# Another order for the first batch of a fused chunked-attention and MLP kernel

## The chip, the core and the metric

The kernel runs on one core of one Trainium2 chip. The core has five engines that run side by side and meet at semaphores: TensorE (PE: matmuls, and transposes done as matmuls), VectorE (DVE), ScalarE (ACT), GpSimd (POOL) and SyncE (SP). Loads and stores are issued from the queues of SP, ACT and POOL and carried out by 16 DMA engines. The metric is the device time of one execution in microseconds. Lower is better.

## The reference

Inputs are q, k, v of shape 4 x 8 x 768 x 64 (batch, heads, sequence, head size), eight memory rows per head for keys and values, and the weights of an MLP (512 to 2048 to 512). The sequence is cut into chunks of 32 queries. A chunk sees the memory rows, 16 rows to its left, its own 32 and 8 to its right. Then comes an MLP with a snake activation.

```python
for c in range(768 // 32):
    l, r = max(0, 32*c - 16), min(768, 32*c + 32 + 8)
    k_full = concat(mem_k, k[:, :, l:r]);  v_full = concat(mem_v, v[:, :, l:r])
    a = softmax(0.125 * q[:, :, 32*c:32*c + 32] @ k_full.T)
    out[:, :, 32*c:32*c + 32] = a @ v_full
x = out with heads side by side              # 3072 x 512
h = x @ w_in                                 # 3072 x 2048
g = h + sin(alpha * h)**2 / (alpha + 1e-9)
y = g @ w_out                                # 3072 x 512
```

## The kernel before

The attention of a batch is computed in blocks of 96 queries, three chunks each, which share one window of 128 keys: 64 rows of K, 8 memory rows, 56 rows of K (`vw` holds V in the same windows). Eight such blocks make a sequence.

Batch 0 has a form of its own, in *units*: a unit is a pair of heads (0 to 3) and a half of the sequence (0 or 1), four blocks each, so there are eight units. In the names below "10" is pair 1, half 0. K and Q of pairs 0, 1 and 2 arrive in fp32 by the queues of SP and ACT (`kq_f`, lines 748 and 756 to 758) and are cast to bf16 (`do_a`, line 683). Pair 3 of both arrives cast by GpSimd's queue (`load_one`, line 191). Every pair is turned on TensorE (`turn`, line 312) and copied from PSUM into `kT` and `qT` (lines 323 and 332). Then, unit by unit, `u_scores` makes the mask and the scores in a pair of PSUM banks (lines 350 and 358) and their exponentials `pt` on ScalarE (line 365). `u_values` multiplies by V (line 377), and `normed` divides on VectorE (a reciprocal, line 386, and a multiplication, line 387) into `x_blk`. `u_turn` turns `x_blk` back on TensorE (line 399) and copies it into `xT` on ScalarE or VectorE (line 402). V comes by GpSimd's queue, one pair of heads per word in two or three transfers (`load_v`, lines 204 to 217), and `put_memv` writes the eight memory rows of V into every window (line 224).

After that there are four stages, one for each batch. A stage computes the batch's MLP and, between its matmuls, the attention of the next batch. The first MLP matmul has 16 tiles of 128 rows of d_ff. A tile has two halves of 384 tokens and each half accumulates four parts (kt 0 to 3, one per pair of heads; line 457) in a pair of PSUM banks. Then come a sine on ScalarE (line 472), a square on one of three engines (lines 477 and 480) and the sum `gT` on VectorE (line 484). The second matmul is at line 495 and its stores at line 505.

The order of all this is written out by hand in the table `WORDS`: one text for the front (batch 0's attention) and one for each stage. Each word calls a method `do_` plus its first letter, and every engine executes its instructions in the order in which the words emit them. The words that matter here are:

- y and z: zero matmuls that keep TensorE busy, of 128 and 512 columns (lines 725 and 719)
- Cb, Ck, Cl, Cm and others: constants (masks, memory keys, alpha); Cv, Cz, Cp, Cs are memsets on GpSimd
- a4A: cast of tile 4 (0 to 3 are K's pairs, 4 to 7 Q's) on ScalarE; a last letter V means VectorE
- k0, l0: turns of K's and Q's pair 0; K0A, L0V: their copies, with the engine
- s10, v10, T10, t10: scores, values and turn of unit 10, the copy on ScalarE (T) or VectorE (t)
- V024: V of batch 0, heads 2 and 3; m0: the memory rows of V; dq068: a load of Q, batch 0, heads 6 and 7
- I02: w_in tiles 0 and 1; Ws, We: loading of the sine or the exponential table on ScalarE
- p0 and P0: parts 0 to 2 of MLP tile 0, first and second half; b0 and h0: the rest of that half

PSUM has eight banks of 512 fp32 columns. `Banks` hands out single banks and pairs, the one that was given back first ahead of the others, so another order of the words gives other banks.

The front before loads V of pairs 1, 0, 3, 2 in this order and takes the values in the order 11, 10, 01, 00, 31, 30, 21, 20.

Of the kernel before, what the change touches and what calls it, by code (L numbers as in the profile page):

```python
# [17 lines left out]
ALU = mybir.AluOpType  # L18
# [1 line left out]

WORDS = (
    (
# [4 lines left out]
    ),  # L27
    (
# [93 lines left out]
def kernel(  # L122
# [12 lines left out]
    nc = tc.nc  # L135
# [5 lines left out]
    HP = H // 2  # L141
    FT = d_ff // P
    KT = d_model // P
# [173 lines left out]
    def copier(eng):  # L317
        return {"A": nc.scalar.copy, "V": nc.vector.tensor_copy, "P": nc.gpsimd.tensor_copy}[eng]
# [136 lines left out]
    def half_tile(t, hf, k0=0, k1=4):  # L455
        for kt in range(k0, k1):
            nc.tensor.matmul(  # L457
                t["hT"][:, hf, 0:HALF],
                w_in_sb[:, kt, P * t["ft"]:P * t["ft"] + P],
                t["xT"][:, kt, HALF * hf:HALF * hf + HALF],  # L460
                start=(kt == 0), stop=(kt == KT - 1),
            )

    def opened(ft, xT):
        hT, bs = banks.pair()
        return {"ft": ft, "xT": xT, "hT": hT, "bs": bs, "from": [0, 0]}
# [66 lines left out]
    kq = (k_bf, q_bf)  # L533
    todo = [(hp, half) for hp in range(HP) for half in range(2)]

    class Stage:
# [29 lines left out]
        def early(self, a, hf):  # L566
# [3 lines left out]
            half_tile(t, hf, 0, 3)  # L570
            t["from"][hf] = 3

        def do_p(self, a):
            self.early(a, 0)

# [106 lines left out]

        def do_a(self, a):
            hp = int(a[0]) % HP
            dst = kq[int(a[0]) // HP]
            copier(a[1])(  # L686
                dst[:, 2 * hp:2 * hp + 2].rearrange("p h r d -> p h (r d)"), kq_f[int(a[0])][:]
            )

        def do_C(self, a):  # L690
            consts_of[a]()
# [50 lines left out]
    kq_f = [mlp.tile([P, 2, 6 * D], F32, name="kq_f", tag=t) for t in ("u", "s2") * 4]  # L742
# [146 lines left out]
```

## Time and profile before

| | us |
|---|---|
| median of 3 runs | 214.41 (214.40 to 214.45) |
| profiled execution | 214.68 |
| its span, first to last instruction | 212.8 |
| first MLP matmul of batch 0 starts | 24.78 |

| engine | busy us | share of the span |
|---|---|---|
| TensorE | 204.9 | 96% |
| ScalarE | 143.7 | 68% |
| VectorE | 139.9 | 66% |
| GpSimd | 100.9 | 47% |

In the profile's rows a timeline row gives start, duration, engine, line, operation, tile written and tiles read, and in brackets the idle time before it and what ended that. "q" behind an engine's name is its sequencer, which issues DMAs. A row of a group ends with busy time, mean ns of one, and idle time before it with its releasers. A row of DMA issues gives count, size and the microseconds from issue to landing. A row of the chain of waits gives start, duration and what held the end back at that time. Neighbouring rows of one kind are merged ("x8").

### The profile page before, as it was taken

The page shows a single profiled execution, that of the slowest core. Times are in us where ns is not written, and L with a number is a line of the kernel's source. Part 1 is how long each engine was busy: PE and PEld are TensorE (multiplying, and loading weights), DVE is VectorE, ACT ScalarE, POOL GpSimd, SP SyncE. Part 2 cuts the span into 40 slices and gives each one's busy share as a digit, 9 for nine tenths or more (in the row PEclk, how much of TensorE's full clock was granted, in tenths as well). Part 3 has the DMA queues.
Part 4 walks back from the last instruction along what each step waited for, and adds up shares of the span by engine and source line. Part 5 has one row for each costly group of instructions (what it writes and reads, how often), then busy time and mean ns, then how long its engine had stood idle before and what let it go on. Part 6 is the DMA issues. An engine that isn't in the chain of part 4 may idle for free.

```text
span 212.8 us, 4568 instructions
## 1 busy us (share of the span) xinstructions
PE 204.9 (96%) x1772; PEld 118.1 (55%) x1772; DVE 139.9 (66%) x210; ACT 143.7 (68%) x229; POOL 100.9 (47%) x142
## 2 busy tenths in 40 slices
PE   7879999999999999999999999999999999999994
PEld 7456665565455556555455555554555555554453
DVE  4788788999452749976766649897247187865010
ACT  2579898978848469968837199887856189891110
POOL 8998605589697297109795048664000022200000
PEclk9999999999999999999999999999999999999999
DMA  5999999999999999999999259999944400000312
GB/s 156 332 158 139 212 207 204 205 139 183 131 160 155 176 114 129 121 144 146 146 152 183 74 125 125 137 157 133 134 104 107 137 0 0 3 2 0 148 52 99
DMA packets 95853, 27.82 MB, mean 131 GB/s; under 512 B 84808, under 2 KB 92376, under 8 KB 95832
## 3 DMA queue, kind: packets, MB, share of 16 engines
q0 software_dynamic: 69152, 13.64, 89.3%
q1 hardware_dynamic: 25720, 12.68, 29.6%
q10 hardware_dynamic: 960, 1.21, 1.7%
q8 instruction: 14, 0.23, 0.6%
q14 instruction: 7, 0.06, 0.1%
HBM read 29.66 MB, written 6.29 MB: 169 GB/s over the span
## 4 chain that ended last, share of the span: by engine, by line
PE 78%; DVE 8%; ACT 5%; DMA 4%; issue 3%; SPq 1%; DVEq 0%; ACTq 0%
PE ps L495 39%; PE ps L457 30%; DMA kq_f<-in_k_dram 4%; PE ps L447 3%; DVE gT L484 2%; PE ps L418 2%; DVE x_blk L387 2%; DVE s L480 2%; ACT s L477 2%; PE ps L399 1%; ACT pt L365 1%; PE ps L312 1%; ACT u L472 1%; DVE q_bf L686 1%; DVE rinv L386 0%
## 5 line engine op out<-in xcount | busy, mean ns | idle before, releaser
L495 PE MATMUL ps<-w_out_sb,gT 128*128 128x512 bf16 (+1 forms) x400 | 89.1, 371 | 0.0
L457 PE MATMUL ps<-xT,w_in_sb 128*128 128x384 bf16 x512 | 85.9, 326 | 0.6 <-DVE gT L484 0.4
L484 DVE SCALAR_TENSOR_TENSOR gT<-s,inv_alpha,ps 128x768 bf16<-128x768 f32 x64 | 63.1, 1012 | 12.3 <-ACT s L477 5.2
L457 PEld LDWEIGHTS <-w_in_sb 128*128 128x128 bf16 x512 | 49.7, 98 | 35.2 <-issue 2.0
L472 ACT ACTIVATE u<-ps,alpha_sb 128x768 f32<-128x768 f32 x64 | 56.6, 894 | 16.9 <-PE ps L457 14.4
L495 PEld LDWEIGHTS <-gT 128*128 128x128 bf16 x400 | 37.1, 98 | 37.1 <-DVE gT L484 0.2
L480 POOL TENSOR_TENSOR s<-u 128x768 f32<-128x768 f32 x11 | 17.2, 1568 | 67.2 <-ACT u L472 56.4
L432 ACT ACTIVATE pt<-ps,biasm 128x256 bf16<-128x256 f32 x72 | 27.1, 488 | 10.5 <-PE ps L418 10.5
L502 DVE COPY o_sb<-ps 128x512 f32<-128x512 f32 (+1 forms) x15 | 10.0, 669 | 27.6 <-PE ps L495 25.7
L480 DVE TENSOR_TENSOR s<-u 128x768 f32<-128x768 f32 x23 | 21.9, 953 | 7.6 <-ACT u L472 7.5
L477 ACT ACTIVATE s<-u 128x768 f32<-128x768 f32 x30 | 25.0, 841 | 0.5
L387 DVE TENSOR_TENSOR x_blk<-ps,rinv 96x512 bf16<-96x512 f32 x32 | 22.0, 687 | 1.1
L502 ACT COPY o_sb<-ps 128x512 f32<-128x512 f32 (+1 forms) x10 | 5.7, 572 | 22.0 <-PE ps L495 22.0
L208 POOL DMA_DIRECT2D vw<-in_v_dram x13 | 12.0, 926 | 6.3 <-PE ps L399 5.4
L386 DVE RECIPROCAL rinv<-ps 96x8 f32<-96x8 f32 x32 | 6.4, 199 | 13.1 <-PE ps L447 12.7
L215 POOL DMA_DIRECT2D vw<-in_v_dram x13 | 13.3, 1024 | 1.6 <-DMA vw<-in_v_dram 1.6
L274 POOL DMA_DIRECT2D kst<-in_k_dram x16 | 13.0, 815 | 1.8 <-DMA vw<-in_v_dram 1.2
L268 POOL DMA_DIRECT2D kst<-in_k_dram x16 | 11.1, 691 | 2.1 <-DMA kst<-in_k_dram 1.0
L281 POOL DMA_DIRECT2D q_bf<-in_q_dram x12 | 10.7, 911 | 0.0
L402 ACT COPY xT<-ps 128x384 bf16<-128x384 bf16 x10 | 5.0, 496 | 8.2 <-PE ps L399 8.2
L447 PEld LDWEIGHTS <-pt 128*128 128x128 bf16 x192 | 8.2, 97 | 4.2 <-ACT pt L432 0.3
L447 PE MATMUL ps<-vw,pt 128*128 128x65 bf16 x192 | 8.9, 193 | 0.0
(83 smaller groups left out, 140.7 us busy)
## 6 DMA issues: line engine op xcount, KB each, us to landing
out_dram<-o_sb SPq DMA_DIRECT2D x23, 256.0 KB, 2.2
q_bf<-in_q_dram POOLq DMA_DIRECT2D x12, 128.0 KB, 7.7
kq_f<-in_k_dram SPq DMA_DIRECT2D x3, 384.0 KB, 6.2
kq_f<-in_q_dram ACTq DMA_DIRECT2D x3, 384.0 KB, 7.9
w_in_sb<-in_moe_w_in_dram POOLq DMA_DIRECT2D x1, 1152.0 KB, 12.9
vw<-in_v_dram POOLq DMA_DIRECT2D x7, 128.0 KB, 7.7
vw<-in_v_dram POOLq DMA_DIRECT2D x8, 112.0 KB, 8.1
kst<-in_k_dram POOLq DMA_DIRECT2D x14, 64.0 KB, 5.5
```

The source lines that it names most:

```text
L215: nc.gpsimd.dma_start(vw[72:128, c0:hi, 0:D], win(vflat, base + QW * c0 + 48, hi - c0, 56))
L274: nc.gpsimd.dma_start(kst[72:72 + n, j, :].rearrange("p (h d) -> p h d", d=D), k[b, :, QW * j + 48:QW * j + 48 + n, :].rearrange("h p d -> ...
L387: nc.vector.tensor_tensor(out=x_blk[:].rearrange("p g e d -> p e g d"), in0=otv[0:QW, :, :, 0:D], in1=rinv[:].unsqueeze(3).to_broadcast([Q ...
L432: nc.scalar.activation(pt[:, 0:H * QW].rearrange("p (g e c) -> p g e c", g=2, e=4)[:, :, :, 32 * m:32 * m + 32], sc[:, :, 0:4 * QW].rearra ...
L447: nc.tensor.matmul(otv[:, e, hp, :], pt[:, QW * i:QW * i + P], vws[b % 2][:, 2 * hp + e, j, 0:D + 1],)
L457: nc.tensor.matmul(t["hT"][:, hf, 0:HALF], w_in_sb[:, kt, P * t["ft"]:P * t["ft"] + P], t["xT"][:, kt, HALF * hf:HALF * hf + HALF], start= ...
L472: nc.scalar.activation(t["u"][:], t["hT"][:, :, 0:HALF], ACTF.Sin, scale=alpha_sb[:, ft:ft + 1])
L477: nc.scalar.activation(s2[:], u[:], ACTF.Square)
L480: e.tensor_tensor(out=s2[:], in0=u[:], in1=u[:], op=ALU.mult)
L484: nc.vector.scalar_tensor_tensor(out=gT[:, ft, :].rearrange("p (e c) -> p e c", e=2), in0=t["s2"][:], scalar=inv_alpha[:, ft:ft + 1], in1= ...
L495: nc.tensor.matmul(o[:, c0:c1], gT[:, ft, P * s:P * s + P], w_out_sb[:, ft, c0:c1], start=(ft == 0), stop=(ft == FT - 1),)
L502: copier(state["engines"][state["o"] % len(state["engines"])])(o_sb[:, c0:c1], o[:, c0:c1])
```

## The change

Only the front's order, one cast's form and one unused method are changed. The texts of the four stages stay as they are.

- V is loaded by pairs 0, 1, 2, 3, and the values are taken in that order.
- K's pair 0 and Q's pair 0 are cast first on ScalarE, and Q's pair 1 on VectorE (before: the cast of K's pair 2 stood ahead of it). VectorE's three casts, now of Q's pairs 1 and 2 and K's pair 2, are written as a maximum of the tile with itself, an operation with two inputs, in place of a copy.
- The memory rows of V (m0) go from ahead of VectorE's casts to between them. Pair 1's Q is copied by VectorE, pair 3's K by VectorE, pair 2's Q by VectorE.
- GpSimd's memsets change places: Cp goes ahead of K's load of pair 3, Cv and Cz behind the first V load.
- There are fewer zero matmuls at the very start; between the memory keys and the first turn stand one wide and 24 narrow ones, where there were six wide ones.
- The sine table is loaded ahead of four of ScalarE's five turn copies, where it stood behind all of them.
- Parts 0 to 2 of MLP tile 0 are issued in the front: those of the first half ahead of the turn of unit 31, the last one, and those of the second half behind it. Stage 0's b0 and h0 then have only part 3 left.
- `do_j` is new, and no word calls it.

```diff
 WORDS = (
     (
-        'y1 y1 y1 Ci y1 a4A We y1 Cb a1A y1 y2 y1 y1 dq068 Cl y1 Cm y1 Cf z1 z1 eVA z1 eVA a0A Ck m0 Cz z1 '
-        'dk068 Cp V024 z1 z1 V002 z1 a2V V068 z1 z1 Cv l0 z1 a5V z1 L0A k1 k0 z1 k2 l1 K1A V046 K0A a6V L1A '
-        's00 s10 s11 K2V l2 k3 L2V K3A s01 v11 dm l3 L3A v10 s20 v01 s30 v00 s31 v30 s21 v31 z1 T01 v20 T30 '
-        'I02 Cs T00 v21 t10 T20 t31 z1 t11 I27 t21 Ws '
+        'y1 z1 z1 y1 y1 Cb Cm z1 y1 a0A Cl z1 z1 Ci eVA y1 a4A dq068 Cp dk068 Ck a1A z1 y1 Cf y1 y1 y1 y1 y1 '
+        'a5V k0 z1 k1 V002 l1 L1V K1A We K0A Cv Cz z1 l0 V024 z1 z1 L0A a6V y1 z1 s10 s00 m0 s01 l3 l2 k3 s11 '
+        'a2V k2 K2A K3V V046 L3A y1 y1 L2V v00 s21 V068 v01 s20 v10 s30 v11 T10 t01 s31 v20 y1 Ws T00 v21 T20 '
+        'dm v30 z1 I02 T21 v31 t11 Cs z1 T30 I27 p0 t31 P0 '
     ),
@@
         def do_a(self, a):
             hp = int(a[0]) % HP
-            dst = kq[int(a[0]) // HP]
-            copier(a[1])(
-                dst[:, 2 * hp:2 * hp + 2].rearrange("p h r d -> p h (r d)"), kq_f[int(a[0])][:]
-            )
+            dst = kq[int(a[0]) // HP][:, 2 * hp:2 * hp + 2].rearrange("p h r d -> p h (r d)")
+            src = kq_f[int(a[0])][:]
+            if a[1] == "V":
+                nc.vector.tensor_tensor(out=dst, in0=src, in1=src, op=ALU.max)
+            else:
+                copier(a[1])(dst, src)
```

More of the change, by code (lines that the diff above doesn't have):

```diff
@@ L571, in early, with do_j @@
             t["from"][hf] = 3
+        def do_j(self, a):
+            if int(a) not in self.tile:
+                self.tile[int(a)] = opened(int(a), self.next_x())
+            t = self.tile[int(a)]
+            half_tile(t, 0)
+            t["from"][0] = KT
         def do_p(self, a):
```

## The prediction

> **What bounds the kernel now.** I read the page's busy line first, then the chain of waits over the first 25 us, then the timelines of VectorE, ScalarE and TensorE in that stretch, then the DMA rows of V.
>
> ```profile
> PE 204.9 (96%) x1772; PEld 118.1 (55%) x1772; DVE 139.9 (66%) x210; ACT 143.7 (68%) x229; POOL 100.9 (47%) x142
> ...
> PEclk9999999999999999999999999999999999999999
> ...
> L457 PE MATMUL ps<-xT,w_in_sb 128*128 128x384 bf16 x512 | 85.9, 326 | 0.6 <-DVE gT L484 0.4
> ```
>
> TensorE is busy for 96% of the span, and in front of all 512 first-MLP matmuls together it idled 0.6 us. So what follows the first of them is TensorE's own work, and the span is: the moment at which that stream starts, plus work that the change leaves alone. What sets that moment is in the chain:
>
> ```profile
> 2.57 8.45 DMA kq_f<-in_k_dram
> ...
> 11.61 1.68 DVE q_bf L686
> ...
> 14.60 2.22 ACT pt L365 x3
> ...
> 24.95 2.62 PE ps L457 x16
> ```
>
> Loads of K and Q to 11.0, VectorE's casts to 13.3, the exponentials from 14.6, then VectorE's eight normalizations, one behind the other, to 24.4, the turns, and the MLP. Sixteen matmuls take 2.62 us, 0.164 us each. VectorE in that stretch:
>
> ```profile
> 9.36 1.22 DVE L224 COPY vw<-memv_st 8x4096 bf16<-8x4096 bf16 x1
> 11.05 0.56 DVE L686 CAST k_bf<-kq_f 128x768 bf16<-128x768 f32 x1 [0.47 <-DMA kq_f<-in_k_dram]
> 11.52 3.15 DVE L686 CAST q_bf<-kq_f 128x768 bf16<-128x768 f32 x2
> 14.60 0.94 DVE L323 COPY kT<-ps 128x768 bf16<-128x768 bf16 x1
> ...
> 17.41 0.20 DVE L386 RECIPROCAL rinv<-ps 96x8 f32<-96x8 f32 x1 [0.35 <-PE ps L377]
> 17.64 0.69 DVE L387 TENSOR_TENSOR x_blk<-ps,rinv 96x512 bf16<-96x512 f32 x1
> ...
> 23.70 0.69 DVE L387 TENSOR_TENSOR x_blk<-ps,rinv 96x512 bf16<-96x512 f32 x1
> 24.31 1.14 DVE L402 COPY xT<-ps 128x384 bf16<-128x384 bf16 x4
> ```
>
> The same cast took 0.56 once and 3.15 for two: something held those two up by about 1 us each. The eight multiplications, each with its reciprocal, come every (23.70 - 17.64)/7 = 0.87 us. TensorE and ScalarE:
>
> ```profile
> 1.20 4.45 PE L725 MATMUL ps<-zeros 128*128 128x128 bf16 x40 [1.20 <-DVE tiny L762]
> 8.29 1.47 PE L719 MATMUL ps<-zeros 128*128 128x512 bf16 x6
> 13.33 0.53 PE L312 MATMUL ps<-ident,q_bf 128*64 128x128 bf16 x12 [1.01 <-DVE q_bf L686]
> 21.29 0.43 PE L377 MATMUL ps<-vw,pt 128*128 128x65 bf16 x8
> 24.78 17.40 PE L457 MATMUL ps<-xT,w_in_sb 128*128 128x384 bf16 x104
> ...
> 43.21 0.53 PE L312 MATMUL ps<-ident,k_bf 128*64 128x128 bf16 x12
> ...
> 8.41 1.56 ACT L686 CAST k_bf<-kq_f 128x768 bf16<-128x768 f32 x2 [1.07 <-DMA kq_f<-in_k_dram]
> ...
> 22.14 1.48 ACT L402 COPY xT<-ps 128x384 bf16<-128x384 bf16 x3
> 24.64 1.28 ACT L738 ACT_TABLE_LOAD   x1
> ```
>
> So the ninth MLP matmul starts at 24.78 + 8 x 0.164 = 26.09. That is the mark against which I measure.
>
> **The change, part by part.** First the transfers of V, each pair of heads a long row block and a short one:
>
> ```profile
> 9.19 1.83 POOL L215 DMA_DIRECT2D vw<-in_v_dram  x1
> ...
> 12.03 0.87 POOL L215 DMA_DIRECT2D vw<-in_v_dram  x1
> ...
> 14.28 0.86 POOL L215 DMA_DIRECT2D vw<-in_v_dram  x1
> ...
> vw<-in_v_dram POOLq DMA_DIRECT2D x1, 112.0 KB, 8.3
> ...
> vw<-in_v_dram POOLq DMA_DIRECT2D x1, 112.0 KB, 7.5
> ...
> vw<-in_v_dram POOLq DMA_DIRECT2D x1, 112.0 KB, 7.1
> ```
>
> Landing is issue plus the last column: second pair 9.19 + 8.3 = 17.5, third 12.03 + 7.5 = 19.5, fourth 14.28 + 7.1 = 21.4. Every one is issued 7 us ahead of landing and they come 2 us apart, so the DMA engines are the limit and not GpSimd's issue. The change reorders heads, not bytes; the n-th pair still lands then. Moving the 8 small memsets, the column of ones and the zero columns of kT past V's issues shifts issues by at most 1.5 us inside that lead: nothing, unless the lead is gone, then up to that 1.5.
>
> Casts with two inputs. A maximum of a tile with itself moves fp32 through VectorE as the squares do, which stand beside GpSimd's issues here:
>
> ```profile
> 46.85 0.95 DVE L480 TENSOR_TENSOR s<-u 128x768 f32<-128x768 f32 x1
> ...
> 47.07 1.00 POOL L208 DMA_DIRECT2D vw<-in_v_dram  x1
> ```
>
> 0.95 beside an issue, so I take 0.95 for each of three; the ends are 0.56 (the free cast) and 1.6 (the mean of the held ones). Two held casts get 1.2 us cheaper together, the third 0.4 dearer.
>
> The order, walked with those durations (an operation of VectorE starts some 0.08 ahead of the shown end of the one in front, 11.05 + 0.56 against 11.52):
> - The Q cast of pair 1 goes ahead of everything else on VectorE. Its tile is loaded by 9.1:
>
> ```profile
> 2.12 0.49 ACTq L748 DMA_DIRECT2D kq_f<-in_q_dram  x1
> ...
> kq_f<-in_q_dram ACTq DMA_DIRECT2D x1, 384.0 KB, 7.0
> ```
>
> (2.12 + 7.0.) VectorE's constants end at 9.36 now, behind an alpha transpose that waits for 40 zero matmuls (4.45 us); in the new order 16 narrow ones and three of 512 columns, 16 x 0.111 + 3 x 0.44 = 3.1, stand ahead of it, so they end between 8.0 and 9.4. I take 8.7; the memory rows (1.22) have gone behind. Cast 9.2 to 10.15, transposes 0.53, copy of qT 0.96: 11.73; now the cast alone ends at 13.3.
> - ScalarE casts K0, Q0, K1 as they land, three at 0.8, and copies kT1, kT0, qT0 (0.8 each too) to 12.45. First exponential 12.45 instead of 14.60; four, at 2.22/3 = 0.74, end at 15.4. It stays ahead of VectorE from there.
> - VectorE after 11.73: cast Q2 0.95, memory rows 1.22, cast K2 0.95, kT3 0.94, qT2 0.96, less five overlaps of 0.08: first reciprocal at 16.35, against 17.41. The memory rows were in a gap at 9.36 and now cost their full 1.22 here; this is counted. Here it takes 1.22 beside an issue of GpSimd (9.19) that is stretched to 1.83, so I take 1.22; the upper end is 1.22 + 1.0, by the held casts. The Trainium skill (SBUF — State Buffer, "Who interferes with whom") speaks against taking that for granted: copies and casts in a two-port mode and GpSimd's operations hold one port pair in turn, and whichever starts first keeps the other out for its whole length. By it this copy would cost up to one issue more, and 1.22 is then luck of the start.
> - Values in the order of landing, 0.87 a unit: pair 0 from 16.35 to 18.1, pair 1 (landed 17.5) to 19.8, one turn copy 1.14/4 = 0.28 to 20.1, pair 2 (19.5; its PSUM banks are free at 19.8, eight matmuls 0.43) from 20.2 to 21.95, pair 3 (21.4, matmuls to 21.9) to 23.7. VectorE and V's transfers end together here: either can hold it. Now it is 24.39.
> - The load of the sine table, 1.28, moves ahead of four of ScalarE's turn copies: 20.6 to 22.05 with its small activation, then four copies at 0.49 to 24.0. Now it ends at about 26.1, just as the eighth MLP matmul does, and the first sine begins; with an earlier matmul it would be late where it stands, so its move is needed and not a gain of its own. The copies are not late: unit 30 is turned at 22.85.
> - First parts of tile 0: three matmuls (p0) behind the third copy, at 23.5; the turn of the last unit at 24.0; three more (P0) at 24.2 to 24.7, in which VectorE makes the last copy (0.34); the fourth parts 24.7 to 25.02. Four of the six lie in time that TensorE would have idled. These need the first w_in block, 15.78 + 6.9 = 22.7. Tile 4 is wanted at 26.3; its block lands at 17.64 + 8.1 = 25.7:
>
> ```profile
> 15.78 0.81 POOL L249 DMA_DIRECT2D w_in_sb<-in_moe_w_in_dram  x1
> ...
> 17.64 1.51 POOL L249 DMA_DIRECT2D w_in_sb<-in_moe_w_in_dram  x2
> ...
> w_in_sb<-in_moe_w_in_dram POOLq DMA_DIRECT2D x1, 256.0 KB, 6.9
> ...
> w_in_sb<-in_moe_w_in_dram POOLq DMA_DIRECT2D x1, 640.0 KB, 8.1
> ```
>
> Ahead of them TensorE has fewer zero matmuls; they are filler and cost nothing while it waits.
>
> The ninth MLP matmul starts at 25.0 instead of 26.1: 1.1 us less. What could take a gain back later are loads that do not move. The tightest is K of batch 1, issued at 22.13 and 19.5 on its way, landed at 41.6:
>
> ```profile
> 22.13 0.89 POOL L191 DMA_DIRECT2D k_bf<-in_k_dram  x1
> ...
> k_bf<-in_k_dram POOLq DMA_DIRECT2D x1, 768.0 KB, 19.5
> ```
>
> It is first transposed at 43.2, and at 42.1 then: that holds by 0.5 us. I round the gain to 1.0. The profiled execution took 214.68 (its span 212.8), so 213.7, span 211.8; the median of the runs is 0.27 below that execution: **213.4**.
>
> **Rivals.** About 0.43 us (0.2%) is the least that a measurement of this kernel tells from no change.
>
> A: the gain is half eaten. V's last transfers stay the end of the chain, or land late by half a microsecond: the last blocks take 7.1 to 8.3 us to land, a spread of 1.2, and the normalizations start as they land with no slack for pairs 1 and 3. Then 0.5 of the 1.0 is lost: 213.9. For it: the exact tie above. Against: that spread is in the landing times that I used.
>
> B: no change. VectorE's memory rows, now between the casts, are held by GpSimd's issues as the two casts were. 1.0 on the chain takes the whole gain: 214.4. For it: two of the three casts here were held. Against: the 1.22 beside a GpSimd issue.
>
> C: slower. TensorE's clock stays low for longer. The PEclk row shows full speed in all 40 slices, but the durations do not: 40 zero matmuls of 128 columns in a row run at 0.111 us each from 1.20 to 5.65, and afterwards 512 columns take 0.245, not 0.44: it has sped up to about double near 6. The changed front has 12 such and two wide ones, and then waits on mcol, alpha and the memory keys, by my walk some 0.5 us of gaps before 6.2. If the speed-up comes only after 12, 24 filler matmuls take 2.6 instead of 1.3 and three sets of transposes twice 0.53 each: the Q1 transposes end at 12.9 instead of 10.7. VectorE's chain hangs on them: 2.2 later, 1.1 lost in the end: 215.6. It decides from about 9 us; before that the transposes wait for the casts anyway. For it: that is the one thing that the front loses. Against: behind the gap of 1.01 us ahead of 13.33 twelve transposes take 0.53, 0.044 each, so gaps do not bring the slow rate back at once. The Trainium skill (TensorE: Matmul & The Clock Gate, "The HAM clock gate") states that the clock is released after a window of about 3.4 us in which the array is busy, and that these windows run free of the kernel's start; by it, one missed window would put the release at 9.4, just at the edge. No row here shows a missed window.
>
> **How the numbers follow.** The forecast, 1.0 less, 0.58; A 0.14; B 0.12; C 0.16 (with any other loss, such as casts at 1.6). Faster is the forecast and A: 0.72; same B: 0.12; slower C: 0.16. The likeliest case alone: the casts at 0.56 rather than 0.95 would bring it at most 0.4 more before V's landing holds, so 213.0 to 213.8. The range for 8 in 10 takes in A and B, and the near part of C: 212.9 to 214.9.
>
> **What would show it.** Three two-input casts at 0.95 with GpSimd issuing beside them; first exponential near 12.5; first reciprocal near 16.4; last normalization ending near 23.7; first MLP matmul near 23.5, the ninth near 25.0, and the stream unbroken from there. Wrong if the first reciprocal is later than 17.4, if a normalization waits for V after 21.9, if the zero matmuls are still at 0.11 us behind 9 us, or if TensorE shows a new wait for a load behind 42 us.

## The result, and the profile after

| | before | after |
|---|---|---|
| median, us | 214.43 | 215.55 |
| lowest and highest, us | 213.89 to 215.97 | 213.88 to 217.16 |
| profiled execution (span) | 214.68 (212.8) | 215.58 (213.7) |
| ninth MLP matmul starts | 26.09 | 27.0 |

The ratio is 1.0043, 95% interval 1.0023 to 1.0062: the change makes the kernel slower by 0.4%. Forecast were 213.4 and a range of 212.9 to 214.9, so sign and range are both wrong. One of the 22 executions of the change, the one of 217.16, ran in a slower state, and the ratio and the counts below leave it out.

The chain of waits in the trace of the change (start, duration, what held the end back at that time) shows the new front:

```profile
2.12 8.56 DMA kq_f<-in_q_dram
...
10.71 0.97 DVE q_bf L695
...
11.72 0.55 PE ps L312 x12
...
12.29 0.96 DVE qT L332
13.25 0.88 DVE q_bf L695
...
14.15 1.22 DVE vw L224
...
15.39 0.91 DVE k_bf L695
...
16.34 0.96 DVE kT L323
17.30 0.70 DVE qT L332
...
18.29 0.47 PE ps L358 x8
18.76 0.37 PE ps L377 x8
...
19.23 0.22 DVE rinv L386
```

Every link of the forecast's walk is there and in its order, and the two-input casts take the forecast's time. But the chain begins with a load of Q that ends at 10.7, and the walk began at 9.2. TensorE's timeline shows the other end of the front:

```profile
6.84 2.77 PE L734 MATMUL ps<-zeros 128*128 128x128 bf16 x24
...
11.72 0.53 PE L312 MATMUL ps<-ident,q_bf 128*64 128x128 bf16 x12 [0.58 <-DVE q_bf L695]
...
25.52 0.65 PE L457 MATMUL ps<-xT,w_in_sb 128*128 128x384 bf16 x3
26.00 0.34 PE L399 MATMUL ps<-ident,x_blk 96*128 96x96 bf16 x4
26.18 16.91 PE L457 MATMUL ps<-xT,w_in_sb 128*128 128x384 bf16 x101
```

Three MLP matmuls, the last turn, and then the stream. The ninth MLP matmul is the sixth of the last row: 26.18 + 5 x 0.164 = 27.0. From there to the end of the span it is 213.7 - 27.0 = 186.7, and before it was 212.8 - 26.09 = 186.7. So what differs is the start of the stream, as the forecast's frame had it.

### The profile page after: what moved, and what is told of

It is laid out like the page before. It is cut to its first block, busy times and chain, and to the rows that moved or that the text cites. A ratio compares the mean times of both kernels' runs of the same rounds, so it can differ in the third digit from the quotient of the medians.

```text
span 213.7 us, 4567 instructions
## 1 busy us (share of the span) xinstructions
PE 205.5 (96%) x1763; PEld 119.1 (56%) x1783; DVE 139.3 (65%) x210; ACT 143.5 (67%) x229; POOL 100.4 (47%) x142
## 4 chain that ended last, share of the span: by engine, by line
PE 80%; DVE 6%; ACT 5%; DMA 4%; issue 2%; ACTq 1%; DVEq 0%
PE ps L495 39%; PE ps L457 34%; DMA kq_f<-in_q_dram 4%; PE ps L447 3%; PE ps L418 2%; DVE gT L484 1%; PE ps L399 1%; ACT s L477 1%; ACT u L472 1%; DVE s L480 1%; DVE q_bf L695 1%; DVE qT L332 1%; ACT qT L332 1%; DVE x_blk L387 1%; PE ps L312 1%
## 5 line engine op out<-in xcount | busy, mean ns | idle before, releaser
L495 PE MATMUL ps<-w_out_sb,gT 128*128 128x512 bf16 (+1 forms) x382 | 86.9, 370 | 1.3 <-issue 0.3
L432 ACT ACTIVATE pt<-ps,biasm 128x256 bf16<-128x256 f32 x72 | 27.2, 489 | 10.5 <-PE ps L418 10.5
L502 DVE COPY o_sb<-ps 128x512 f32<-128x512 f32 (+1 forms) x15 | 10.0, 669 | 27.4 <-PE ps L495 25.6
```

Of the source, the lines that this page charges most:

```text
L432: nc.scalar.activation(pt[:, 0:H * QW].rearrange("p (g e c) -> p g e c", g=2, e=4)[:, :, :, 32 * m:32 * m + 32], sc[:, :, 0:4 * QW].rearra ...
L495: nc.tensor.matmul(o[:, c0:c1], gT[:, ft, P * s:P * s + P], w_out_sb[:, ft, c0:c1], start=(ft == 0), stop=(ft == FT - 1),)
L502: copier(state["engines"][state["o"] % len(state["engines"])])(o_sb[:, c0:c1], o[:, c0:c1])
```

## The experiments

Two theories stood at the start. L, the landing: the change makes the load of Q's pair 1 the start of the whole chain, and that load lands later than one trace of before showed. K, the clock: TensorE's clock is low for longer (the forecast's rival C). A third question, opened by the first results, is what the two-input casts are worth.

Beside the times, each timed execution has a mean granted clock of TensorE. It is either 0.997 to 1.000 or at most 0.992, and in the traces of the low ones there is one stretch of 3.4 us at half clock. That makes it possible to count executions with such a stretch.

**The change again, and a third trace of it** (no edit).

> The changed kernel as it is, for a second profile. Theory L (landing): the front hangs on the landing of Q's pair 1, 10.7 us in the profile of the changed kernel and 9.1 in that of the kernel before; VectorE's cast of that tile starts within 0.1 us of the landing, and the ninth MLP matmul comes 16.3 us after it (27.0 against 10.7), whatever the clock does. Theory K (clock): TensorE's speed-up came one window late (24 narrow zero matmuls took 2.77 us behind 6.8), and the ninth matmul follows the end of the Q1 transposes only through that. By L a landing back at 9.2 gives a ninth matmul near 25.5 and some 1.4 us less; by K it changes nothing unless the zero matmuls speed up. Time about 215.5, 0.2 to 0.6% above the kernel before.

> The change, unchanged, for a third trace. Theory L: Q's pair 1 lands between 9.5 and 10.7, its cast starts at the same moment, and the ninth MLP matmul stands 16.2 to 17.1 us behind that start.

Measured: the first 215.64, ratio 1.0069 (1.0046 to 1.0093), its trace 215.42 with a span of 213.6; the other, timed once, 214.60 with 212.7. VectorE's timeline in the first trace, and a row of TensorE's behind it:

```profile
9.76 0.96 DVE L695 TENSOR_TENSOR q_bf<-kq_f 128x768 bf16<-128x768 f32 x1 [1.95 <-DMA kq_f<-in_q_dram]
...
17.37 0.19 DVE L386 RECIPROCAL rinv<-ps 96x8 f32<-96x8 f32 x1
...
19.05 0.20 DVE L386 RECIPROCAL rinv<-ps 96x8 f32<-96x8 f32 x1 [0.76 <-PE ps L377]
```

```profile
18.30 0.28 PE L358 MATMUL ps<-qT,kT 64*128 64x96 bf16 x5 [0.55 <-issue]
```

VectorE's in the third trace:

```profile
9.49 0.96 DVE L695 TENSOR_TENSOR q_bf<-kq_f 128x768 bf16<-128x768 f32 x1 [1.69 <-DMA kq_f<-in_q_dram]
...
16.86 0.19 DVE L386 RECIPROCAL rinv<-ps 96x8 f32<-96x8 f32 x1
...
18.23 0.20 DVE L386 RECIPROCAL rinv<-ps 96x8 f32<-96x8 f32 x1 [0.45 <-PE ps L377]
```

The three traces against the forecast's walk, in us:

| | walk | trace 1 | trace 2 | trace 3 |
|---|---|---|---|---|
| Q pair 1's cast starts | 9.2 | 10.71 | 9.76 | 9.49 |
| first reciprocal | 16.35 | 18.08 | 17.37 | 16.86 |
| second reciprocal | 17.22 | 19.23 | 19.05 | 18.23 |
| last normalization ends | 23.7 | 25.83 | 25.64 | 24.83 |
| ninth MLP matmul | 25.0 | 27.0 | 26.8 | 26.0 |

From the cast to the first reciprocal it is 7.37, 7.61 and 7.37 (walk: 7.15), whenever the cast starts: the chain follows the landing. From the first to the second reciprocal it is 1.15, 1.68 and 1.37 (walk: 0.87). The values of the second unit stand behind the scores of pair 2 on TensorE, and those wait for VectorE's last copy ahead of the first reciprocal. In traces 2 and 3 TensorE also stands still inside these scores for 0.55 and 0.18 us, with nothing to wait for that the profile shows ("issue"). The rest is as walked.

Of the 33 timed executions of the change (both series), 10 have a stretch at half clock. Their mean is 216.3 and 216.4 in the two series, that of the others 215.1 and 215.5. Of 92 timed executions of before beside the experiments none has one. Executions with a half-clock stretch are thus 0.9 to 1.2 us longer, three of ten of them, which makes 0.3 on the mean. A later landing in the same executions may be a part of that; the series cannot tell. The larger part of the loss is there without them.

**The opening zeros of before.** More narrow zero matmuls at the very start, as before the change:

```diff
-        'y1 z1 z1 y1 y1 Cb Cm z1 y1 a0A Cl z1 z1 Ci eVA y1 a4A dq068 Cp dk068 Ck a1A z1 y1 Cf y1 y1 y1 y1 y1 '
+        'y1 y1 y1 y1 y1 Cb y1 y2 y1 y1 Cm y1 a0A Cl y1 z1 z1 Ci eVA z1 a4A dq068 Cp dk068 Ck a1A z1 y1 Cf y1 y1 '
```

> The changed kernel with the opening zero matmuls of the kernel before: 40 narrow ones ahead of the mask and alpha transposes, fewer narrow ones behind the memory keys. K: full speed near 6 us again, the K0 transposes in 0.53 instead of 0.82, and the whole front earlier: 1 us or more below the changed kernel, 214.4 or less. L: the clock is fast early, but the chain still starts at the landing of Q's pair 1: within 0.3 us of the changed kernel.

Measured: 215.26, ratio 1.0046 (1.0026 to 1.0066), against 215.64 for the change on the same chip; one of 12 executions at a low clock. By this series the zeros are worth 0.4 at most, about the share of the half-clock stretches (against the first series of the change, 1.0043, they are worth nothing), and they do not undo the loss.

**The memory rows ahead of the casts** (m0 right behind the memory keys).

```diff
-        ... Ck a1A z1 y1 Cf y1 y1 y1 y1 y1 '
+        ... Ck a1A z1 y1 Cf m0 y1 y1 y1 y1 y1 '
-        ... s10 s00 m0 s01 l3 l2 k3 s11 '
+        ... s10 s00 s01 l3 l2 k3 s11 '
```

> The changed kernel with the memory rows of V (1.22 us on VectorE) moved from between the casts to behind the small constants, where VectorE is idle from 7.8 to 10.7. L: that copy leaves the chain; the first reciprocal comes 1.2 earlier behind the landing of Q's pair 1 (6.2 us instead of 7.4), and the ninth matmul 0.6 to 1.2 earlier, the rest taken by V, whose pair 1 landed at 18.2. Time 214.3 to 214.9. Rival: V's landing holds all of it, and nothing changes.

Measured: 215.79, ratio 1.0054 (1.0027 to 1.0081): no gain. Four of 11 executions had the low clock, the profiled one among them. The 1.2 us off VectorE's chain came back as a wait for TensorE, which ran at half clock just then. VectorE's timeline, TensorE's two waits ahead of it, and busy time of the engines by stretch (the column behind POOL is the granted clock):

```profile
17.16 0.96 DVE L323 COPY kT<-ps 128x768 bf16<-128x768 bf16 x1 [2.75 <-PE ps L312]
```

```profile
9.63 0.53 PE L312 MATMUL ps<-ident,k_bf 128*64 128x128 bf16 x12 [0.83 <-ACT k_bf L697]
11.06 0.63 PE L312 MATMUL ps<-ident,q_bf 128*64 128x128 bf16 x12 [0.90 <-DVE q_bf L695]
```

```profile
11.30:14.60 3.30, 3.30 (x31) 1.61 (x26) 2.69 (x3) 1.27 (x2) 3.27 (x5) 0.51 2.25 158
```

The seven executions at full clock have a median of 214.77, so without the clock this edit might gain; that was not separated further.

**Q's pair 1 loaded first.** The loads on ScalarE's queue in the order 1, 0, 2, and ScalarE's casts of K's pair 1 and Q's pair 0 exchanged.

```diff
-        load_f(nc.scalar, q, hp, kq_f[4 + hp])
+        qp = (1, 0, 2)[hp]
+        load_f(nc.scalar, q, qp, kq_f[4 + qp])
-        ... Ci eVA y1 a4A dq068 Cp dk068 Ck a1A z1 y1 Cf ...
+        ... Ci eVA y1 a1A dq068 Cp dk068 Ck a4A z1 y1 Cf ...
```

> The changed kernel with Q's pair 1 loaded ahead of Q's pair 0, and the cast of K1 ahead of that of Q0 on ScalarE. L: the tile lands near 6.2, its cast runs at 7.8, and the Q1 transposes then wait for K's pair 1 alone (10.6 to 11.2): the qT copy at 11.7 instead of 12.3, 0.6 less at the end, 214.9. K: the transposes are held by the slow clock until 10, so nothing changes: 215.5.

Measured: 214.19, ratio 0.9996 (0.9974 to 1.0018); 1.45 less than the change on the same chip. No execution of 12 had a low clock. VectorE's timeline:

```profile
7.83 0.96 DVE L695 TENSOR_TENSOR q_bf<-kq_f 128x768 bf16<-128x768 f32 x1
...
10.96 0.96 DVE L332 COPY qT<-ps 128x768 bf16<-128x768 bf16 x1 [2.17 <-PE ps L312]
```

TensorE's, between the two:

```profile
10.06 0.53 PE L312 MATMUL ps<-ident,k_bf 128*64 128x128 bf16 x12 [1.25 <-ACT k_bf L697]
```

VectorE's cast no longer waits for a load. What is late next is K's pair 1, whose turn stands ahead of that of Q on TensorE. This edit takes back the whole loss.

**Q's pair 1 loaded last** (order 0, 2, 1, words as in the change): the same lever pushed the other way.

> The change, with the ACT queue's loads of Q in the order 0, 2, 1: Q's pair 1 lands third, near 12.0, instead of second, 9.5 to 10.7. Theory L: its cast starts 1.3 to 2.5 us later, near 12.0; the Q pair 2 cast then has its tile and saves 0.3; the whole chain moves by 1.0 to 2.2: 216.5 to 217.7, with the ninth MLP matmul near 28.5. Theory K (the landing is covered, and the loss is TensorE's clock alone): 215.6, ninth matmul near 27.0.

Measured: 218.97, ratio 1.0222 (1.0192 to 1.0252), more than theory L said. VectorE, TensorE and the stretch behind them:

```profile
11.84 0.96 DVE L695 TENSOR_TENSOR q_bf<-kq_f 128x768 bf16<-128x768 f32 x1 [4.04 <-DMA kq_f<-in_q_dram]
```

```profile
12.85 0.53 PE L312 MATMUL ps<-ident,q_bf 128*64 128x128 bf16 x12 [2.62 <-DVE q_bf L695]
```

```profile
13.70:17.10 3.40, 3.40 (x31) 1.88 (x33) 3.34 (x4) 0.82 (x2) 3.40 (x5) 0.50 3.23 140
```

The cast starts 1.1 to 2.3 later than in the three traces of the change, the chain follows, and TensorE is idle for 2.62 us in one piece; 0.8 us behind that its clock falls to half for 3.4 us. All 5 executions had a low clock, three of them as low as two such stretches would make it (0.982 to 0.984). So L and K hang together: the later this tile lands, the longer TensorE idles, and more executions have a half-clock stretch. Counted over all series of the new front: tile first, 0 of 48 executions (four kernels); last, 5 of 5; second, as in the change, 10 of 33, and 10 of 41 in its variants (zeros first 1 of 12, memory rows ahead 4 of 11, and, below, plain casts 2 of 12 and no early parts 3 of 6). The kernel before has none in 92, and with two-input casts 2 of 24.

The Trainium skill (TensorE: Matmul & The Clock Gate, "HAM oscillation — how this bites in real kernels") gives the rule that TensorE must not idle for more than about 3.4 us. Here shorter waits were enough: half clock followed a wait of 2.62 us, in the kernel with the early memory rows two waits of 0.83 and 0.90, and in the one without the early parts two of 1.00 and 0.94. The longest single wait does not decide: with plain casts (below) TensorE waited 1.52 us in one piece and kept its clock.

```profile
10.02 0.53 PE L312 MATMUL ps<-ident,k_bf 128*64 128x128 bf16 x12 [1.52 <-ACT k_bf L693]
```

Added up from 8 to 13 us, TensorE was idle for 1.73, 1.93 and 3.19 us in the three traces with a stretch, and for 0.1 to 1.67 us in the other fifteen. Whether the sum decides, or when the waits come, no run separates.

**Plain copies as casts**, the change otherwise kept.

```diff
-            if a[1] == "V":
-                nc.vector.tensor_tensor(out=dst, in0=src, in1=src, op=ALU.max)
-            else:
-                copier(a[1])(dst, src)
+            copier(a[1])(dst, src)
```

> The changed kernel with VectorE's three casts as plain copies again. If GpSimd's issues hold a plain cast as in the kernel before (1.6 instead of 0.96 each), the chain gets up to 2 us longer: 216 to 217.5. If they run free in the new places (0.56 each), it gets up to 1.2 shorter: 214.4. One held and two free is the likeliest, since GpSimd waits for a free transfer slot from 11.6 to 13.3: 215.2 to 215.8.

Measured: 214.66, ratio 1.0011 (0.9983 to 1.0038). VectorE's casts:

```profile
10.08 0.56 DVE L693 CAST q_bf<-kq_f 128x768 bf16<-128x768 f32 x1 [2.26 <-DMA kq_f<-in_q_dram]
...
14.75 0.77 DVE L693 CAST k_bf<-kq_f 128x768 bf16<-128x768 f32 x1
```

Plain casts are not held for a microsecond here. By the ratios (1.0011 against 1.0043 and 1.0069, the first of these with an interval that overlaps) the two-input form costs the change 0.7 to 1.2 us; the cast that starts the chain explains 0.96 - 0.56 = 0.4 of it.

**The two-input casts alone**, in the kernel before, in two series with a trace each.

```diff
-            copier(a[1])(dst, src)
+            if a[1] == "V":
+                nc.vector.tensor_tensor(out=dst, in0=src, in1=src, op=ALU.max)
+            else:
+                copier(a[1])(dst, src)
```

> The kernel before with the three VectorE casts written with two inputs and nothing else changed. There the chain ran through them: 0.56 + 3.15 becomes 3 x 0.96, some 0.8 us less on VectorE, and the values can start that much earlier: 213.5. Rival: the values of the first pairs then wait for V (pair 0 landed at 17.5, third in order there), and less than 0.3 is left.

> The kernel before with two-input casts, once more, for a second trace. In the first trace the front was 0.4 us earlier than before and 0.9 us were lost behind 100 us in two waits. If these waits are chance, they are absent here, the sines behind the front run 0.3 to 0.5 us ahead to the end, and the time is 214.1. If they are a consequence of the earlier front, they stand at the same places (near 101 and 168 us) and the time is 214.9.

Measured: 214.98, ratio 1.0018 (1.0002 to 1.0034), and 215.05, ratio 1.0025 (1.0006 to 1.0044): a small loss, where the forecast's 1.2 - 0.4 = 0.8 us was to be gained. The first trace has its ninth matmul at 25.7, 0.4 earlier than before, but TensorE then lost 0.5 us at 101 and 0.4 at 168, the latter in a wait for a tile of `xT` that a DMA turns for the last batch:

```profile
168.75 3.41 PE L457 MATMUL ps<-xT,w_in_sb 128*128 128x384 bf16 x20 [0.26 <-DMA xT<-x_blk]
```

Both are absent from the second trace, and the series takes the same time, so they are not the reason. The second trace's ninth matmul is at 26.2, no earlier than before, since K's pair 2 landed later (VectorE's first cast waits 0.94 for it). (The second wait is there in six of the 18 traces, worth 0.15 to 0.4 us, and none of the six is one of the change's three.) VectorE's timeline in the second trace:

```profile
11.53 0.96 DVE L688 TENSOR_TENSOR k_bf<-kq_f 128x768 bf16<-128x768 f32 x1 [0.94 <-DMA kq_f<-in_k_dram]
12.40 1.82 DVE L688 TENSOR_TENSOR q_bf<-kq_f 128x768 bf16<-128x768 f32 x2
```

The casts take what the forecast said. What was wrong must be the price of the casts that they replace.

**The kernel before, three more traces.**

> The kernel before, unchanged, for another trace. Theory T (its own trace was untypical, and the two held casts of 3.15 us were chance): the two Q casts take 1.2 to 2.0 together, and the first reciprocal is at 16.6 to 17.1, not at 17.4. Theory U (typical): 2.8 to 3.2 again and 17.4.

> The kernel before, a further trace. As the last; and by theory L Q's pair 1 lands anywhere from 9.2 to 10.7 without moving the end, since its cast stands behind K's pair 2 here.

> The kernel before, a further trace. By theory T two Q casts in 1.2 to 2.0 us together, by theory U in 2.8 to 3.2.

Measured, timed once each: 215.02, 215.38 and 214.60 (spans 213.2, 213.5 and 212.8). The load of Q's pair 1, VectorE's casts of Q with the first reciprocal, and TensorE's first values, in the first of them (views: DMA issues, VectorE's timeline, TensorE's timeline):

```profile
kq_f<-in_q_dram ACTq DMA_DIRECT2D x1, 384.0 KB, 7.8
```

```profile
11.83 0.54 DVE L686 CAST q_bf<-kq_f 128x768 bf16<-128x768 f32 x1
12.72 0.77 DVE L686 CAST q_bf<-kq_f 128x768 bf16<-128x768 f32 x1 [0.35 <-DMA kq_f<-in_q_dram]
...
17.01 0.20 DVE L386 RECIPROCAL rinv<-ps 96x8 f32<-96x8 f32 x1 [0.87 <-PE ps L377]
```

```profile
16.49 0.41 PE L377 MATMUL ps<-vw,pt 128*128 128x65 bf16 x8 [0.64 <-DMA vw<-in_v_dram]
```

The same in the second:

```profile
kq_f<-in_q_dram ACTq DMA_DIRECT2D x1, 384.0 KB, 7.7
```

```profile
11.35 1.34 DVE L686 CAST q_bf<-kq_f 128x768 bf16<-128x768 f32 x2
```

```profile
16.81 0.42 PE L377 MATMUL ps<-vw,pt 128*128 128x65 bf16 x8 [1.10 <-DMA vw<-in_v_dram]
```

And in the third:

```profile
kq_f<-in_q_dram ACTq DMA_DIRECT2D x1, 384.0 KB, 8.4
```

```profile
11.84 0.54 DVE L686 CAST q_bf<-kq_f 128x768 bf16<-128x768 f32 x1
12.69 0.56 DVE L686 CAST q_bf<-kq_f 128x768 bf16<-128x768 f32 x1 [0.32 <-DMA kq_f<-in_q_dram]
```

Two readings. First, the two Q casts take 1.31, 1.34 and 1.10 us, not 3.15: the holding that the forecast wanted to remove is there in one of four traces. GpSimd's timeline tells them apart. In before's own trace it works without a pause from 11.01 to 15.14, beside both casts. In the three others it waits, ahead of a transfer of V, for its load of Q's pair 3 to land, 0.74, 0.50 and 1.61 us; the last of these:

```profile
13.13 0.87 POOL L215 DMA_DIRECT2D vw<-in_v_dram  x1 [1.61 <-DMA q_bf<-in_q_dram]
```

The four casts that start in such a wait take 0.54 to 0.56, so whether a cast is held seems to hang on a landing too. (K's pair 2, 0.56 in before's own trace, took 0.94 and 0.89 in the first and third of these, beside an issue.) Where they are quick, the first pair of V or the loads hold the front instead (0.64 and 1.10 us ahead of the first values), so a quicker cast would gain little even then. Second, Q's pair 1 lands at issue (2.13) plus 7.8, 7.7 and 8.4: 9.9, 9.8 and 10.5. With the two traces of before with two-input casts (10.2 and 10.0), before's own, and the seven in which the new front loads it second (9.5 to 10.7), there are 13, and the 9.1 on which the forecast's walk rested is the earliest of them all. Before did not care: this tile's cast stood behind that of K's pair 2, which lands at 11.

**Without the early first parts** (p0 and P0 left out, so the first tile is computed whole behind the last turn).

```diff
-        'dm v30 z1 I02 T21 v31 t11 Cs z1 T30 I27 p0 t31 P0 '
+        'dm v30 z1 I02 T21 v31 t11 Cs z1 T30 I27 t31 '
```

> The changed kernel without the early parts of MLP tile 0; its eight matmuls then all stand behind the last turn. By the prediction's step four of six matmuls lay in idle time: 0.66 us more, 216.2. Rival: they only push the last turn and its copy back, and nothing changes.

Measured: 216.93, ratio 1.0101 (1.0077 to 1.0125), with three of six executions at a low clock. The early parts are a gain, of 0.7 to 1.2 us by the ratios. In its trace the ninth matmul stands 1.55 behind the last normalization, against 1.17 with them; that is 0.4. A wait for `xT` near 170 us, as above, adds 0.3 in this trace, and three low clocks of six instead of ten of 33 would be 0.2 on the mean of the series; why the series shows as much as it does stays open.

**Pair 1 first and the memory rows ahead**, and both kernels with Q's pair 1 first once more with plain casts. The loads and ScalarE's casts are as in "Q's pair 1 loaded first"; the other words of the first:

```diff
-        'a5V k0 z1 k1 V002 ... s10 s00 m0 s01 l3 l2 k3 s11 '
+        'a5V m0 k0 z1 z1 z1 z1 k1 V002 ... s10 s00 s01 l3 l2 k3 s11 '
```

> The changed kernel with Q's pair 1 loaded first, the memory rows of V copied right behind that tile's cast while VectorE waits for the transposes, and three more wide zero matmuls in TensorE's wait for K's pair 1. By theory L the first reciprocal comes near 15.6 instead of 16.95 with Q's pair 1 first alone, V's last pair (21.4) becomes the bound, and the ninth matmul comes near 25.0 to 25.2: span 211.8, 213.4 to 213.7, faster than both kernels. Rival: V lands later than the chain is ready by more, and it stays at the 214.2 of Q's pair 1 first alone.

> The reordered load of Q's pair 1, the memory rows ahead, and plain copies for casts. Where the Q pair 1 cast starts at 7.9 instead of 9.7 or later it has 1 us to spare, and of the three casts only those of pair 2 (Q2, K2) lie on VectorE's chain. Theory L (the chain starts with the landing of Q pair 1; a two-input cast costs 0.96 where a free plain one costs 0.56): two casts by 0.4 less, half of it eaten by waits for TensorE, so 0.3 us below the same kernel with two-input casts (213.9): 213.6. Rival H (plain casts are held by GpSimd's issues, as two of three were before, 1.6 each): 1.0 more, 214.9 or above.

> The reordered load of Q's pair 1 and plain copies, the memory rows where the change put them. Theory L: 0.3 us below the same with two-input casts (214.2): 213.9. If the memory rows ahead are what made the other faster, it lies 0.3 above that one; if not, level with it. Rival H: above 215.0.

| Q's pair 1 first, and | us | ratio to before |
|---|---|---|
| memory rows where the change has them, two inputs | 214.19 | 0.9996 (0.9974 to 1.0018) |
| memory rows ahead, two inputs | 213.92 | 0.9972 (0.9953 to 0.9991) |
| memory rows ahead, plain | 214.09 | 0.9993 (0.9977 to 1.0010) |
| memory rows between, plain | 214.04 | 0.9987 (0.9970 to 1.0004) |

The second row is the only kernel here that beats both others, by 0.3% in its series; the four are not told apart from one another. Plain casts gain nothing once this tile is early (213.6 was expected): the cast that started the chain has time to spare, and with the memory rows ahead their own copy was stretched. VectorE in that kernel's trace:

```profile
7.83 0.76 DVE L693 CAST q_bf<-kq_f 128x768 bf16<-128x768 f32 x1
8.62 1.88 DVE L224 COPY vw<-memv_st 8x4096 bf16<-8x4096 bf16 x1
```

The profiled execution of the faster kernel (213.5 of span, 215.32) is the slowest of its 12, and shows rival C in the form that the forecast gave it. TensorE, then VectorE:

```profile
6.84 2.77 PE L734 MATMUL ps<-zeros 128*128 128x128 bf16 x24
9.54 0.83 PE L312 MATMUL ps<-ident,k_bf 128*64 128x128 bf16 x12
```

```profile
12.18 0.96 DVE L332 COPY qT<-ps 128x768 bf16<-128x768 bf16 x1 [1.94 <-PE ps L312]
```

24 zero matmuls at 0.115 each, and K's transposes in 0.83 and not 0.53: slow until about 10, and here, where nothing else was late, the copy behind them waited 1.94 us. In the first trace of the change the same 24 took the same 2.77, but Q's tile was later still and covered it.

## Why the prediction was wrong, step by step

**The frame** held: in twelve of the 18 traces the span is the ninth MLP matmul's start plus 186.7, to a tenth, and the change's three are among them. The other six are longer by 0.2 to 0.9, by the late waits above. No load that follows 42 us took anything back from the change.

**"Its tile is loaded by 9.1 ... Cast 9.2"** is the step that failed. The change put a load at the head of the chain that had been 2 us off it, and the forecast took its landing from one execution as a fixed time. In the change's three traces the cast starts 1.51, 0.56 and 0.29 later, 0.8 on average. Loading that tile first brought the time back to that of before, loading it last made it 3.3 to 3.8 us worse than the change, by the ratios, a part of which is the half clock.

**"Two held casts get 1.2 us cheaper together"** failed in the same way. The two-input form measured 0.95 or 0.96 each time, as forecast. But 3.15 us for the two plain ones was that execution's; three others have 1.1 to 1.3. Against these, the two-input form loses 0.4 on the cast at the head of the chain. This saving is no term of the walk, which takes 0.95 for each cast; it was a reason to expect that the new front would beat the old one. The Trainium skill (SBUF — State Buffer, "Who interferes with whom"), by which a copy in a two-port mode can be held by GpSimd while an operation with two inputs waits only for GpSimd's reads, agrees with both findings: two-input casts took 0.95 or 0.96 in every trace, plain ones between 0.54 and 1.75 (the slower one of the 3.15). How often a hold happens is another question: in these four traces it went with the landing that GpSimd waited for, and no edit tests that.

**The walk from there** was short by 0.3 up to the first reciprocal, and by 0.5 between the first and the second (1.15, 1.68 and 1.37 in place of 0.87). Around the memory rows at least two of the five overlaps of 0.08 did not happen, and in the second trace VectorE waited 0.23 for Q's pair 2. The walk's 11.73 is a slip, as its terms give 9.2 + 0.95 + 0.53 + 0.96 = 11.64; the first trace takes 2.54 for these three steps, so the slip happened to stand for the time between them. The first exponential came at 14.48, 13.53 and 13.26 and not at 12.45, but stayed ahead of VectorE. "0.87 a unit" is VectorE's pace, but the second unit's values are queued on TensorE behind scores that need VectorE's last copy. From the second unit on the walk is right to 0.1. The order of the values, the sine table and the early parts behaved as forecast: no values waited for V in any of the three traces, and the early parts are a real gain.

**Rival C** was given 0.16 and is partly what happened, though not by its mechanism. The late release does occur, and was covered in the change's own trace. What goes with lost time is a half-clock stretch behind the idle time in which TensorE waits for Q: 0.3 us on the mean. The forecast's argument against it, that one gap of 1.01 us ahead of the transposes does not slow them, was too weak, because the stretch comes later and only in some executions.

**The last step, "213.7 ... the median of the runs is 0.27 below"**, was a mistake of its own. The front was walked anew from absolute times, and so an offset of the old front's execution says nothing about it.

The sum: late landing 0.8, casts to the first reciprocal 0.3, second unit 0.5, half-clock stretches 0.3, the wrong offset 0.27: 2.2 us, against 215.55 - 213.4 = 2.15. That they agree to a tenth is partly luck, since three traces give the first three terms, and the forecast had rounded its gain from 1.1 down to 1.0.

Against the kernel before the account is looser. Its ninth matmul stands at 26.1, 26.2, 26.6 and 25.6 in four traces, 0.5 ahead of the change's on the mean, and the half-clock stretches add 0.3; the series differ by 1.1 and 1.35. The four traced executions of before took 214.9 on the mean, where its series have medians of 214.25 to 214.52, so the traces show before slower than it mostly is, and which of its steps is quicker in the other executions they do not show.

## What to carry to other kernels

When a change makes a load the start of the chain, its landing time is a distribution and not a number: take it from several executions, or leave it a microsecond of slack, and look at what was hiding it. A duration that differs between equal instructions of one trace (0.56 once, 3.15 for two) is a question to ask of a second trace before anything is built on it. And where TensorE waits for such a load, count its idle time twice: once on the chain, and once more for the clock.

## What the runs showed of the hardware

- A load of 384 KB issued at 2.1 us, with three others of that size issued from 1.2 to 2.2 us, landed at 9.1 to 10.5 us in four traces of one program and at 9.5 to 10.7 in three of another.
- Half-clock stretches of 3.4 us, in the three traces in which TensorE was idle for 1.73 us or more between 8 and 13 us, and in none of fifteen with 1.67 or less. By the granted clock, 10 of 33 executions of the change have one, none of 48 where the load came first, and all 5 where it came last.
- In the four traces of the kernel before, plain casts of 128x768 from fp32 on VectorE took 0.54 to 0.56 us where they started while GpSimd waited, and 1.48 and 1.75 us in the trace in which GpSimd worked on beside them; the two-input form took 0.95 or 0.96 in every trace that has it.
- The granted clock in the profile reads 1.00 also in the stretch in which 128 columns take 0.115 us; the slow start shows in the durations alone.
